# A fused attention and expert kernel whose order is built with other estimates and other weights

## The chip, the cores and the metric

The kernel runs on one core of one Trainium2 chip. The metric is the device time of one execution in microseconds (us). Beside it stands a profile of one execution: what each engine did and when. The engines are PE (matrix multiply; PEld is its loading of weights), DVE (vector), ACT (scalar), POOL (GpSimd) and SP (which issues DMAs here). Each engine takes its instructions in the order in which the program has them; semaphores hold an instruction until what it reads has been written.

## The reference

For 4 batches of 8 heads, 768 positions and 64 channels, attention in which a query sees only keys of the same hash bucket; its output, laid out as 3072 rows of 512, goes through two matrix products with a squared ReLU between them. The core of it:

```python
q_bits = (np.einsum('bhsd,dk->bhsk', q, proj) > 0).astype(np.int64)
k_bits = (np.einsum('bhsd,dk->bhsk', k, proj) > 0).astype(np.int64)
mask = q_bucket[:, :, :, None] == k_bucket[:, :, None, :]
scores = scale * np.matmul(q, k.transpose(0, 1, 3, 2))
scores = np.where(mask, scores, -1000000000.0)
scores = scores - np.max(scores, axis=-1, keepdims=True)
attn = np.exp(scores)
attn = attn / (np.sum(attn, axis=-1, keepdims=True) + 1e-09)
x = np.matmul(attn, v)            # then laid out as (3072, 512)
h = np.maximum(x @ w_in, 0.0)     # (3072, 2048)
out = h * h @ w_out               # (3072, 512)
```

## The kernel before

**The work.** Values that need more than half precision are kept as two f16 parts, a main part and a residual (what is left of the f32 value after the main part); a product is then three matmuls, main by main, main by residual, residual by main. `move` in the code makes a main part, `left` a residual.

*A unit* is 128 queries of one head against its 768 keys. PE writes scores to `pS`; DVE takes the row maximum (`nmx`); ACT takes the exponential with its sum (`e`, `sm`); `rv` is the reciprocal of the sum, one instruction on DVE or POOL and one on DVE; `hl` is the normalised row in two parts, the main one by `move`, the residual by DVE; SP issues a transposing DMA of `hl` into `aT`. Six units (two heads of three) feed one *pair* of attention-value products, `pA` on PE with the values `VV`; its result goes into `xx`, again main part and residual. There are 32 pairs, 192 units.

*An expert stage* takes the four `xx` of 384 rows: for each of 16 blocks of the hidden width 12 matmuls into `pm` (with `win`), a ReLU from `pm` to `g32`, a square in place, the main part of `g` and its residual, and then 9 matmuls into `po` (with `wo`). There are 8 stages. `pm` has one buffer, `g` two. In the first stage the weights `w_in` and `w_out` are still being split into parts, in pieces: `raw` is loaded, `top` and `f` unpack it, `sq` and `pt` find its scale, then come the parts of `win` and `wo`. After the first stage `wo` is scaled in place by `rel`, 16 instructions, before the second stage uses it.

**What sets the order.** The program is not written out in order. Every operation is recorded with the ways in which it can be done (for instance the residual of `g` as a scalar_tensor_tensor on DVE or a tensor_tensor on POOL) and what it depends on. `cost` gives each way a duration in ns, and a planner makes a list schedule of all operations: `forward` starts on each engine what is ready and most urgent, `backward` finds from the schedule how urgent each is, five times over, and the schedule with the shortest planned span is issued. Where an operation has several ways, `forward` compares for each engine when it would be free, plus the operation's cost there times the engine's weight in `PRICE`, plus what is queued ahead; the least wins. DMAs go through one planned queue; a transpose holds SP until the queue is through. DVE and POOL operations that both read the local memory through a shared port are kept apart in the plan (`port`, `held`). In the gaps that the plan leaves on PE before the first expert matmul, `emit` puts filler matmuls (`idle`), one for every 56 ns of 0.6 of the gap. So a number in `cost` or `PRICE` changes which engine does an operation, the order on all engines, and the number of fillers.

Every operation is issued by one line (402; 395 for the fillers, 399 for matmuls recorded as a group), so the profile's rows are told apart by the tiles' names.

Of the kernel before, what the change touches and what calls it, by code (L numbers as in the profile page):

```python
# [13 lines left out]
F32 = mybir.dt.float32  # L14
F32R = mybir.dt.float32r
# [19 lines left out]


BUFS = dict(xx=12, hl=3, raw=2, f=7, e=3, aT=3, g=2, A=2, Q=2, L=2, M=2, RV=2, VV=4)
PRICE = dict(pe=1, dve=3.57, act=0.3, pool=3.06, sp=0.43)
AHEAD, DELAY, LAG = 60, 2500, 1.0

ROUNDS, BEHIND = 4, 40000
# [71 lines left out]
class Program:  # L113
# [59 lines left out]
    @staticmethod  # L173
    def cost(key, name, args, kw):

        size = lambda x: int(np.prod(x.shape[1:]))
        column = {F32: 4 / 2.4, F32R: 0.445}
        if name == "matmuls":

            side = {32: 4, 64: 2}.get(size(args[0][0][1]), 1)  # L180
            t = sum(size(a[2]) * column.get(a[2].dtype, 1 / 2.4) + 7 for a, _ in args) / side
            return t, t
        kinds = [x.rec.kind if isinstance(x, View) else "" for x in args]
        ptr = any(isinstance(x, View) and x.shape[-1] == 1 for x in args[2:3])
        n = max(size(args[0]), size(args[1]) if isinstance(args[1], View) else 0)
        if key == "pe":
            t = max(107, size(args[2]) * column.get(args[2].dtype, 1 / 2.4) + 3)
            return t, t
        if name.startswith("dma"):
            b = int(np.prod(args[0].shape)) * mybir.dt.size(args[0].dtype)  # L190
            inside = name == "dma_start_transpose" or kinds[:2] == ["sb", "sb"]
            busy = 1040 if key == "pool" else (650 if inside else 475) + 50 * (key == "act")
            return busy, b / (175 if name == "dma_start_transpose" else 314)
        if key == "act":
            t = 93 * (isinstance(kw.get("scale"), View) + isinstance(kw.get("bias"), View)) + (51 if "psum" in kinds[:2] else 93) + n / 1.2 + 93 * ("accum_out" in kw)
        elif key == "pool":
            t = 147 + n * (2.1 if args[0].dtype == F32 or args[0].dtype == F32R else 1.88) if name == "tensor_tensor" else 161 + n / 1.2 + 83 * ptr
        else:
            fast = name in ("tensor_copy", "tensor_scalar") and "psum" not in kinds[:2]
            both = len(args) > 3 and isinstance(args[3], View) and args[3].shape[-1] == 1  # L200
            t = 67 + n / (1.92 if fast else 0.96) + 62 * (ptr and (fast or name == "scalar_tensor_tensor")) + 100 * both
        return t, t
# [92 lines left out]
    def forward(self, prio, near):  # L295
# [20 lines left out]
        while True:  # L316
# [25 lines left out]
            if len(o.ways) > 1:  # L342
                for w in o.ways:
                    k2 = w[0].key
                    ahead = sum(ops[j].ways[0][4][0] / len(ops[j].open) for r, j in ready[k2] if ops[j].queue is None and r <= prio[i] + near and j != i)
                    ends[k2] = max(free[k2], t, held if w[5] else 0.0) + w[4][0] * PRICE[k2] + ahead + DELAY * w[1].startswith("dma")
            if any(e < ends[k] and k2 in o.open for k2, e in ends.items()):
# [513 lines left out]
```

## Time and profile before

| | |
|---|---|
| three runs | 923.61, 925.90, 926.62 us, median 925.9 |
| the profiled execution | 925.36 us, of which its span is 923.6 us |
| busy: PE, DVE, ACT, POOL | 885.6, 643.8, 663.6, 54.8 us |
| granted clock of PE, mean | 0.996 |
| first `pm` matmul | starts at 169.50 us |
| last `pA` of the 32 | starts at 822.4 us, last one's matmuls end near 853 |

The span is from the first instruction to the last. A row of groups gives the engine, the operation, what it writes and reads, its shape and count, then after a bar the busy time in us and the mean duration of one in ns, and after a second bar the idle time of that engine just before these instructions, with what ended it. A row of the timeline gives start and duration in us. In the views by stretches each row is one stretch of the span, with its length, then the busy us of PE, PEld, DVE, ACT and POOL, the granted clock, the share of time that DMA packets took, and GB/s. Matmuls are pipelined, and a row's end is modelled; the distance from one start to the next is the better measure of a matmul.

### The profile page before, as it was taken

What the parts mean: (1) busy time and instruction counts of PE and PEld (TensorE: products, weight loads), DVE (VectorE), ACT (ScalarE), POOL (GpSimd) and SP (SyncE); (2) the same over time, 40 slices, a digit from 0 to 9 for tenths busy, and PEclk for the clock granted to TensorE, in tenths of its full rate; (3) what the DMA queues carried; (4) which work ended last, traced back from release to release, by engine and by line L of the source; (5) the groups of instructions that cost most, each with busy time, mean ns of one, the idle gap of its engine ahead of it and who ended that gap; (6) DMA issues with size and microseconds to landing.
All of it is one profiled execution on the core that took longest, in us unless ns stands there. A gap on an engine that the chain in (4) does not pass through costs nothing.

```text
span 923.6 us, 15264 instructions
## 1 busy us (share of the span) xinstructions
PE 885.6 (96%) x5592; PEld 501.3 (54%) x5592; DVE 643.8 (70%) x1206; ACT 663.6 (72%) x1166; POOL 54.8 (6%) x104
## 2 busy tenths in 40 slices
PE   7988988999997999999999999999999999999997
PEld 6555555445554555555555556555555555554553
DVE  5999999988979687889686768797867651211111
ACT  4877987878879677888777768787778673533433
POOL 0111301200103000000000000000000000000000
PEclk9999999999999999999999999999999999999999
DMA  7998999997999797999697959897878640200000
GB/s 236 248 222 210 226 237 213 250 211 193 236 203 242 133 192 148 185 234 244 145 198 159 190 121 198 174 213 154 170 149 177 121 102 10 77 1 0 35 1 35
DMA packets 329323, 149.99 MB, mean 162 GB/s; under 512 B 305568, under 2 KB 305696, under 8 KB 329248
## 3 DMA queue, kind: packets, MB, share of 16 engines
q1 hardware_dynamic: 329248, 149.02, 73.6%
q8 instruction: 44, 0.72, 0.3%
q14 instruction: 31, 0.25, 0.1%
HBM read 43.59 MB, written 6.29 MB: 54 GB/s over the span
## 4 chain that ended last, share of the span: by engine, by line
PE 63%; ACT 5%; DMA 2%; DVE 2%; issue 1%; POOL 0%; SPq 0%; ACTq 0%; DVEq 0%
PE po L402 23%; PE pm L402 21%; PE pS L402 9%; PE pA L399 8%; ACT wo L402 1%; DMA aT<-hl 1%; ACT e L402 1%; PE pd L399 1%; DMA RV<-vp 1%; ACT hl L402 1%; DVE hl L402 1%; ACT g L402 1%; PE pc L402 1%; DVE nmx L402 1%; DMA M<-Q 1%
## 5 line engine op out<-in xcount | busy, mean ns | idle before, releaser
L402 PE MATMUL po<-wo,g 128*128 128x512 f16 x1152 | 332.7, 381 | 2.7 <-ACT wo L402 0.9
L402 PE MATMUL pm<-xx,win 128*128 128x384 f16 x1536 | 322.4, 327 | 1.3 <-DVE g L402 1.0
L402 DVE TENSOR_REDUCE nmx<-pS 128x1 f32<-128x768 f32 x192 | 183.1, 954 | 57.7 <-PE pS L402 56.6
L402 ACT ACTIVATE e<-pS,nmx 128x768 f32<-128x768 f32 x192 | 171.6, 894 | 67.8 <-DVE nmx L402 48.8
L402 DVE SCALAR_TENSOR_TENSOR hl<-e,rv,hl 128x768 f16<-128x768 f32 x192 | 194.1, 1012 | 26.1 <-ACT hl L402 25.5
L402 PEld LDWEIGHTS <-win 128*128 128x128 f16 x1536 | 145.1, 98 | 115.4 <-issue 17.8
L402 ACT ACTIVATE hl<-e,rv 128x768 f16<-128x768 f32 x188 | 173.5, 928 | 25.1 <-ACT e L402 14.0
L402 PEld LDWEIGHTS <-g 128*128 128x128 f16 x1152 | 107.9, 98 | 131.3 <-issue 26.4
L402 DVE SCALAR_TENSOR_TENSOR g<-g,g 128x384 f16<-128x384 f32 x122 | 67.5, 554 | 127.7 <-ACT g L402 127.1
L402 ACT ACTIVATE g<-pm 128x384 f32<-128x384 f32 x125 | 60.7, 486 | 108.3 <-PE pm L402 107.4
L402 ACT ACTIVATE g<-g 128x384 f32<-128x384 f32 (+1 forms) x248 | 128.8, 520 | 10.8 <-PE po L402 5.6
L399 PE MATMUL pA<-aT,VV 128*64 128x384 f16 x1152 | 117.8, 331 | 0.0
L402 PE MATMUL pS<-A,Q 128*128 128x384 f32 x288 | 95.2, 411 | 5.0 <-ACT e L402 4.8
L399 PEld LDWEIGHTS <-VV 128*64 128x64 f16 x1152 | 59.5, 109 | 55.8 <-issue 35.8
L402 PE MATMUL pS<-L,M 128*128 128x384 f32 x288 | 77.8, 350 | 0.2
L402 PEld LDWEIGHTS pS<-A,Q 128*128 128x128 f32 x288 | 49.3, 190 | 29.8 <-ACT e L402 15.9
L402 POOL TENSOR_SCALAR rv<-sm 128x1 f32<-128x1 f32 x74 | 28.8, 389 | 610.6 <-ACT e L402 604.0
L395 PEld LDWEIGHTS <-ones 128*128 128x128 bf16 x756 | 49.9, 103 | 20.1 <-issue 11.8
L395 PE MATMUL idle<-ones 128*128 128x128 bf16 x756 | 54.7, 228 | 2.7 <-DVE ones L402 2.7
L402 PEld LDWEIGHTS pS<-L,M 128*128 128x128 f32 x288 | 51.9, 189 | 3.9 <-issue 2.4
L402 PE MATMUL pS<-Q,M 128*128 128x384 f32 x96 | 37.3, 510 | 9.5 <-ACT e L402 9.1
L402 PE MATMUL pS<-A,L 128*128 128x384 f32 x96 | 36.6, 508 | 5.7 <-ACT e L402 5.4
(92 smaller groups left out, 579.9 us busy)
## 6 DMA issues: line engine op xcount, KB each, us to landing
RV<-vp SPq DMA_DIRECT2D x32, 384.0 KB
R<-kq SPq DMA_DIRECT2D x24, 384.0 KB
raw<-w_in SPq DMA_DIRECT2D x16, 511.8 KB
raw<-w_out SPq DMA_DIRECT2D x16, 511.8 KB
out<-o SPq DMA_DIRECT2D x21, 256.0 KB
Q<-L SPq DMA_DIRECT2D x24, 192.0 KB
Q<-A SPq DMA_DIRECT2D x24, 192.0 KB
L<-M SPq DMA_DIRECT2D x24, 192.0 KB
```

The lines of the kernel that those rows point to most:

```text
L395: issue(q, q.engine.matmul(self.idle[0].real(), self.idle[1].real(), self.idle[1].real(), start=True, stop=True).ins)
L399: ins = q.engine.matmul(*map(real, args), **kw).ins
L402: ins = getattr(q.engine, o.name)(*map(real, o.args), **{k: real(x) for k, x in o.kw.items()}).ins
```

## The change

Four numbers of the planner change: three weights, the bytes per ns of a transposing DMA (175 to 292), and the cost of a POOL operation with one input (161 ns plus 83 for a scale that is a tensor, to 380 ns flat; the part that grows with the size stays).

```diff
-PRICE = dict(pe=1, dve=3.57, act=0.3, pool=3.06, sp=0.43)
+PRICE = dict(pe=1, dve=3, act=1, pool=1.5, sp=0.43)
...
-            return busy, b / (175 if name == "dma_start_transpose" else 314)
+            return busy, b / (292 if name == "dma_start_transpose" else 314)
...
-            t = 147 + n * (2.1 if ... else 1.88) if name == "tensor_tensor" else 161 + n / 1.2 + 83 * ptr
+            t = 147 + n * (2.1 if ... else 1.88) if name == "tensor_tensor" else 380 + n / 1.2
```

What that does to the order is seen on the engines. Three places carry the prediction.

**The end of the first part, on DVE.** Ahead of the sixth `xx` residual, which the first `pm` needs; `top` and `f` unpack weights, `rv` and `hl` are softmax. Before:

```order
L402 SCALAR_TENSOR_TENSOR win<-f,towin,win 128x512 x2
L402 TENSOR_REDUCE nmx<-pS 128x1
L402 SCALAR_TENSOR_TENSOR hl<-e,rv,hl 128x768
L402 SCALAR_TENSOR_TENSOR f<-raw,top_73 128x512
L402 TENSOR_SCALAR top_77<-raw 128x512
L402 RECIPROCAL rv<-rv 128x1
L402 SCALAR_TENSOR_TENSOR xx<-pA,xx 128x384
```

and now:

```order
L402 TENSOR_SCALAR norm<-norm 128x1
L402 SCALAR_TENSOR_TENSOR f<-raw,top_81 128x512
L402 TENSOR_SCALAR norm<-norm 128x1
L402 SCALAR_TENSOR_TENSOR win<-f,towin,win 128x512
L402 TENSOR_SCALAR towo<-norm 128x1
L402 RECIPROCAL rv<-rv 128x1
L402 SCALAR_TENSOR_TENSOR xx<-pA,xx 128x384
```

The `xx` residual was the 304th row of DVE's list (303 instructions and a branch) and is now the 251st; no `top` stands near it, since POOL now has 26 of the 32, where it had 13.

**The scaling of `wo` after the first expert stage.** Before, on ACT, among the exponentials of the next units:

```order
L402 ACTIVATE wo<-wo,rel 128x2x512 x3
L402 ACTIVATE e,sm<-pS,nmx 128x768
...
L402 ACTIVATE wo<-wo,rel 128x2x512
L402 ACTIVATE A<-R,cst 128x768
L402 ACTIVATE hl<-e,rv 128x768
```

and now, on DVE:

```order
L402 TENSOR_SCALAR wo<-wo,rel 128x2x512
L402 RECIPROCAL rv<-rv 128x1
L402 TENSOR_SCALAR wo<-wo,rel 128x2x512 x2
L402 SCALAR_TENSOR_TENSOR hl<-e,rv,hl 128x768
L402 TENSOR_REDUCE nmx<-pS 128x1
```

ACT had 15 of the 16 and DVE one; ACT now has 2, DVE 11 and POOL 3.

**The end of the last stage, on PE.** With the tiles' numbers: the last `pm`, and the `po` matmuls of the last three blocks of the hidden width, each with its own `g`. Before, one `po` of the oldest block and nine of the next stand between the last `pm` and the last block's `g`:

```order
L402 MATMUL pm_10361<-xx_7940,win_726 128x384
...
L402 MATMUL po_9987<-wo_1027,g_10338 128x512
...
L402 MATMUL po_9987<-wo_1027,g_10365 128x512
...
L402 MATMUL po_9987<-wo_1027,g_10386 128x512
```

and now three of the oldest and nine of the next:

```order
L402 MATMUL pm_10143<-xx_7704,win_736 128x384
...
L402 MATMUL po_9767<-wo_1010,g_10122 128x512
L402 LDWEIGHTS g_10122
L402 MATMUL po_9767<-wo_1010,g_10122 128x512
...
L402 MATMUL po_9767<-wo_1010,g_10147 128x512
...
L402 MATMUL po_9767<-wo_1010,g_10168 128x512
```

So PE has two more matmuls to do before it needs the last block's `g`, whose residual is now a tensor_tensor on POOL: 128 of the 128 blocks have it there, where it was 6 (and 122 on DVE).

More of the change, by code (lines that the diff above doesn't have):

```diff
@@ L196, in cost @@
         elif key == "pool":
-            t = 147 + n * (2.1 if args[0].dtype == F32 or args[0].dtype == F32R else 1.88) if name == "tensor_tensor" else 161 + n / 1.2 + 83 * ptr
+            t = 147 + n * (2.1 if args[0].dtype == F32 or args[0].dtype == F32R else 1.88) if name == "tensor_tensor" else 380 + n / 1.2
         else:
```

## The prediction

> **What bounds the kernel now.** I read the page first: busy times, then the two rows that cut the span into 40 slices.
>
> ```profile
> span 923.6 us, 15264 instructions
> PE 885.6 (96%) x5592; PEld 501.3 (54%) x5592; DVE 643.8 (70%) x1206; ACT 663.6 (72%) x1166; POOL 54.8 (6%) x104
> PE   7988988999997999999999999999999999999997
> DVE  5999999988979687889686768797867651211111
> ```
>
> PE looks like the only limit, but its 96% hold two things. The view by stretches, first of all instructions, then of the filler matmuls (tile `idle`) alone, separates them. Columns: length of the stretch, then busy us (and count) of PE, PEld, DVE, ACT, POOL.
>
> ```profile
> 20.00:169.50 149.50, 132.01 (x1084) 82.71 (x1083) 143.20 (x286) 120.54 (x201) 24.64 (x43) 1.00 1.01 229
> 169.50:320.00 150.50, 142.93 (x853) 78.60 (x852) 130.53 (x248) 126.65 (x215) 19.84 (x33) 0.99 0.94 211
> 320.00:900.00 580.00, 577.60 (x3422) 318.29 (x3421) 358.19 (x650) 399.19 (x724) 10.07 (x24) 1.00 0.64 136
> ```
>
> ```profile
> 20.00:169.50 149.50, 42.91 (x631) 1.00 1.01 229
> ```
>
> Up to 169.5 us PE's work is 43 us of filler, and DVE is busy 143.20 of 149.50 us: DVE sets the pace, ACT (120.54) has room. From 320 us on PE is full (577.60 of 580) and DVE has 222 us to spare. Between lies a stretch where both are near full. So the time is (when DVE lets PE get full) plus (what PE still has to do), and an instruction taken from DVE counts only before about 300 us. The timeline shows the hand-over: the sixth `xx` residual on DVE, then the first `pm` matmul on PE.
>
> ```profile
> 168.61 0.53 DVE L402 SCALAR_TENSOR_TENSOR xx<-pA,xx 128x384 f16<-128x384 f32 x1
> 169.06 0.68 DVE L402 SCALAR_TENSOR_TENSOR f<-raw,top 128x512 uint32<-128x512 uint32 x1
> 169.50 1.30 PE L402 MATMUL pm<-xx,win 128*128 128x384 f16 x7
> ```
>
> The rows also show that DVE instructions overlap: 168.61 + 0.53 is 169.14, and the next begins at 169.06. I take 0.05 us off each duration for that.
>
> **The change, part by part.** No arithmetic changes, only who does it and when. The order built from the change has 122 `g` residuals on POOL that were on DVE, 13 more `top` on POOL, 13 more `hl`, 10 of the `wo` scalings moved to DVE, and 216 fewer filler matmuls. The fillers cost nothing themselves: they lie in gaps that DVE makes. The groups' rows price the moves (after the bar: busy us, mean ns):
>
> ```profile
> L402 DVE TENSOR_SCALAR top<-raw 128x512 f16<-128x512 bf16 x19 | 8.8, 463 | 0.4 <-DMA raw<-w_in 0.3
> L402 POOL TENSOR_SCALAR top<-raw 128x512 f16<-128x512 bf16 x13 | 13.4, 1031 | 28.9 <-DMA raw<-w_out 15.3 <-DVE rv L402 6.8 <-DMA raw<-w_in 6.3
> L402 DVE SCALAR_TENSOR_TENSOR g<-g,g 128x384 f16<-128x384 f32 x122 | 67.5, 554 | 127.7 <-ACT g L402 127.1
> L402 POOL TENSOR_TENSOR g<-g,g 128x384 f16<-128x384 f32 x6 | 6.6, 1102 | 10.8 <-ACT g L402 6.0 <-issue 3.7 <-DVE g L402 1.1
> L402 DVE TENSOR_REDUCE rows<-RV 128x12 f32<-128x768 f32 x16 | 15.0, 945 | 6.7 <-ACT RV L402 6.6
> ```
>
> *The first part, DVE's pace.* Up to the sixth `xx` residual DVE's order has 303 instructions before and 250 now. But only the `top` (16 to 5, 11 x 0.463 = 5.1 us) have left the engine; the rest of the 53 (`f`, `win`, `wo` residuals, three units of softmax) is postponed and comes back. So I compare at later points, where the same softmax work is done: at the last `hl` residual that the tenth and the eleventh pair of attention-value products (`pA`) need. At the tenth: 13 `top` fewer (-6.0), 10 `g` residuals fewer (-5.5), `rows` and its like +2.5, small ones +0.3; with 19 overlaps of 0.05 less to take off, -7.8 us. PE's order has by that point 20 more `pm` and 27 more `po` behind it than before, at the steps that these rows show (0.16 and 0.22 us from one start to the next):
>
> ```profile
> 910.05 0.33 PE L402 MATMUL pm<-xx,win 128*128 128x384 f16 x1
> 910.21 0.38 PE L402 MATMUL po<-wo,g 128*128 128x512 f16 x1
> 910.43 0.33 PE L402 MATMUL pm<-xx,win 128*128 128x384 f16 x1
> ```
>
> That is 3.2 + 5.9 = 9.1 us less to do afterwards; together -16.9. At the eleventh: 13 `g` and 13 `top` off, 11 `wo` scalings and 3 `acc` on, -6.2 us; 28 `pm` and 19 `po` ahead, 8.7 us; -14.9. I take the mean, **-15.9**; bounds -20 (nothing is postponed: the 53 instructions' own durations, less the overlaps, sum to 20.4) and -11 (the seventh pair, where the postponed `rows` have come back but few `po` are ahead: -8 and -3).
>
> *The `wo` scalings.* After the first expert stage `wo` is scaled in place, 15 of 16 on ACT:
>
> ```profile
> L402 ACT ACTIVATE wo<-wo,rel 128x1024 f16<-128x1024 f16 x15 | 16.2, 1138 | 0.0
> L402 DVE TENSOR_SCALAR wo<-wo,rel 128x1024 f16<-128x1024 f16 x1 | 0.5, 466 | 0.0
> 260.00:280.00 20.00, 18.34 (x117) 9.85 (x115) 15.29 (x28) 15.77 (x28) 1.63 (x2) 1.00 0.85 193
> 280.00:300.00 20.00, 16.99 (x102) 9.40 (x102) 19.27 (x40) 19.67 (x26) 7.37 (x11) 0.95 1.06 248
> ```
>
> ACT is full there (19.67 of 20) and PE loses 1.66 + 3.01 = 4.7 us, the only real gap after 200 us. Now 11 go to DVE at 0.466, 3 to POOL, 2 stay. I take **-3.5** of the 4.7; bounds 0 and -4.7.
>
> *Port.* 41 wide operations or so come to POOL in the stretch that DVE paces (13 `top`, 14 `g`, the others of `hl`, `A`, `win`, `wo`). When POOL runs, some DVE rows stretch:
>
> ```profile
> 81.50 0.78 POOL L402 TENSOR_SCALAR top<-raw 128x512 f16<-128x512 bf16 x1
> 81.54 1.22 DVE L402 SCALAR_TENSOR_TENSOR wo<-f,towo,wo 128x512 f16<-128x512 f32 x1
> 302.55 1.01 DVE L402 SCALAR_TENSOR_TENSOR hl<-e,rv,hl 128x768 f16<-128x768 f32 x1
> 302.94 1.39 POOL L402 TENSOR_TENSOR g<-g,g 128x384 f16<-128x384 f32 x1 [3.65 <-ACT g L402]
> L402 DVE SCALAR_TENSOR_TENSOR wo<-f,towo,wo 128x512 f16<-128x512 f32 x16 | 12.1, 771 | 0.0
> ```
>
> The `wo` residual that began 0.04 us after POOL took 1.22 instead of 0.77; in the second pair POOL came later and paid itself. I found DVE to be the loser in four of 26 wide POOL operations, some 0.4 us each: 0.065 us an operation, **+2.5** for 41; bounds 0 and +9 (each holds DVE for half its length, half of the time). The Trainium skill's page "SBUF — State Buffer", section "Who interferes with whom", has it as a lock: of GpSimd and a DVE instruction with two SBUF inputs, the one that comes second waits until the other has finished. The rows agree, in both directions.
>
> *`g` residuals, on PE's side.* In the last stages only these stand between `pm` and `po`. The chain after the last matmul of a `pm`:
>
> ```profile
> 907.87 0.49 ACT L402 ACTIVATE g<-pm 128x384 f32<-128x384 f32 x1 [2.29 <-PE pm L402]
> 908.39 1.08 ACT L402 ACTIVATE g<-g 128x384 f32<-128x384 f32 x2
> 909.50 0.56 DVE L402 SCALAR_TENSOR_TENSOR g<-g,g 128x384 f16<-128x384 f32 x1 [3.33 <-ACT g L402]
> 374.65 0.92 POOL L402 TENSOR_TENSOR g<-g,g 128x384 f16<-128x384 f32 x1 [0.22 <-ACT g L402]
> ```
>
> On POOL it takes 0.92 undisturbed, not 0.56, and starts 0.2 later: about 0.55 us late. The order answers with two more `po` matmuls between (front part, last place): 2 x 0.216 = 0.43. Left is 0.1 us for 48 blocks of the last three stages, of which a margin takes most: **+1.5**; bounds 0 and +14 (0.3 each). Behind a late residual PE's whole queue waits. POOL's `rv`, queued behind a `g`, is late by up to 0.92 as well; it is on the path only through the transposes, next.
>
> *Transposes.* Their price falls from 393 KB at 175 bytes/ns (2.25 us) to 292 (1.35 us), so `pA` is put nearer to the unit that feeds it. Three in a row on SP, the `pA` that they feed, and one landing from the chain that ended last:
>
> ```profile
> 408.50 5.21 SPq L402 DMA_TRANSPOSE aT<-hl  x3
> 427.94 0.68 PE L399 MATMUL pA<-aT,VV 128*64 128x384 f16 x6
> 384.29 5.68 DMA aT<-hl
> L399 PE MATMUL pA<-aT,VV 128*64 128x384 f16 x1152 | 117.8, 331 | 0.0
> ```
>
> 5.21/3 = 1.74 us each: the truth lies between the two prices. The last of the three was issued near 412, landed by 418 at the latest, and PE came 10 us later. In the order the PE work between the last score matmul and its `pA` shrinks by up to 9 us for such pairs, so most of that margin goes. I take **+2**; bounds 0 (as before, when `pA` had 0.0 us of idle time ahead of it) and +12 (ten pairs late by 3 x 0.4). The Trainium skill's page "DMA: Bandwidth & Descriptors", section "Latency and other measured facts", gives 261 GB/s for a transpose: 1.51 us as an estimate, also slower than the new price, but by 0.16 instead of 0.39; by it the term would be +1.
>
> Sum: -15.9 - 3.5 + 2.5 + 1.5 + 2 = -13.4. The profiled execution took 925.4 (span 923.6 and 1.8 around it), 0.5 below the median of 925.9: **912 us**.
>
> **Rivals.** *Given back* (921): DVE stays the bound to 320 us, the port takes its +9 and the `wo` scalings load DVE where PE needs it: -11 - 1 + 9 - 1 = -4. For: in 169.5 to 320 DVE is 87% busy, and 11 scalings are added there. Against: DVE loses 0.55 us with every `g`. This is also where the lock rule of the SBUF page would lead if POOL mostly came first.
>
> *Another pace in the head* (924): with DVE lighter, the DMAs hold the units. For: their share is 1.01 in the head. Against: no `pA` waited for one. Then -15.9 falls away, -3.5 + 2 stays.
>
> *Slower* (941): the transposes. PE takes its queue in order; each of the 26 pairs from the sixth on that reaches its `pA` 1.2 us before the tiles land costs 1.2: +31 in place of +2. It decides from 0.6 us a pair on (15.4/26). For: the new price is 0.39 us under the row and three stand in line. Against: margins as that of 10 us.
>
> **How the numbers follow.** Forecast 0.64, its own range 900 to 922 (-25 with the two gains at their ends and no loss; -4 with the losses near theirs); given back 0.14; another pace 0.09; slower 0.13. The range 899 to 926 holds nearly all of the first two and most of the third. What this measurement tells from no change is about 0.3%, 2.8 us. Faster: 0.62 + 0.11 + 0.04 = 0.77; the same 0.08; slower 0.15.
>
> **What would show it.** First `pm` near 150 us (169.5 less the 20 of those 53 instructions), fillers in the proportion of 540 to 756, DVE still above 93% busy until then; `wo` gap in PE under 2 us; DVE `wo`, `win`, `f` residuals with means up by 0.05 to 0.1 us; PE idle before `po` released by POOL `g` under 3 us; `pA` idle time from DMA under 3 us. If `pm` starts near 150 and the span is still over 920, the middle or the transposes took it; if `pm` starts near 165, DVE was not the pace.

## The result, and the profile after

The changed kernel takes **932.8 us** (median of four runs, 932.13 to 933.9); the kernel before takes 925.6 beside it (four runs, 923.61 to 926.62). The ratio is 1.0082 with a 95% interval of 1.0061 to 1.0102: slower by some 7 us, where 13 us faster was forecast. The profiled execution took 933.2 us, of which 931.5 are its span. An execution with a clearly lower granted clock (0.85 or 0.945 where the others have 0.98 to 1.00) is left out of the medians and ratios below.

The head of the page of the changed kernel, its span and the busy times:

```profile
span 931.5 us, 15081 instructions
PE 879.3 (94%) x5375; PEld 487.0 (52%) x5376; DVE 588.2 (63%) x1086; ACT 629.0 (68%) x1117; POOL 211.9 (23%) x273
```

DVE is 56 us lighter and POOL 157 us heavier, as planned. The view by stretches, cut at the first `pm` matmul, which now starts at 153.6 us; then the group of the fillers:

```profile
20.00:153.60 133.60, 118.88 (x851) 69.74 (x850) 121.35 (x227) 106.55 (x180) 34.10 (x58) 0.97 1.09 238
153.60:320.00 166.40, 151.05 (x888) 82.59 (x888) 138.57 (x271) 127.47 (x228) 48.11 (x60) 1.00 0.93 200
320.00:900.00 580.00, 570.53 (x3362) 311.25 (x3361) 318.77 (x571) 374.90 (x679) 123.16 (x144) 1.00 0.64 137
```

```profile
L395 PE MATMUL idle<-ones 128*128 128x128 bf16 x540 | 39.0, 226 | 1.6 <-DVE ones L402 1.6
```

The hand-over comes 16 us earlier. Yet PE stands 15.4 us in the stretch after it (166.40 less 151.05; before 7.6 of 150.50), and 9.5 us from 320 to 900 (before 2.4).

**How far ahead is PE?** Busy time does not answer it, since a matmul that runs alone is booked longer than one in a chain (in the prediction's rows one `pm` alone has 0.33 us, seven in a row 1.30). Counts do. The view by stretches for one tile, from the start to 900 us: first `pm` and `po` before, then the same two after.

```profile
0.00:900.00 900.00, 311.60 (x1488) 1.00 0.76 166
0.00:900.00 900.00, 319.12 (x1104) 1.00 0.76 166
```

```profile
0.00:900.00 900.00, 305.26 (x1464) 0.99 0.76 166
0.00:900.00 900.00, 316.62 (x1086) 0.99 0.76 166
```

At 900 us the change has done 24 `pm` and 18 `po` fewer: 24 x 0.16 + 18 x 0.216 = 7.7 us behind, which is what the spans differ by (7.9). The same count at other times, with 0.30 us for a `pS` matmul and 0.086 for a recorded `pA` (estimates; at 800 and 900 us they play no part, as both kinds are equally far in all rows), gives this table of PE's work ahead of the kernel before (us, each row one profile). The other kernels come below: `half` has lighter transposes, all or some of them, `hl4` a fourth buffer for `hl`, `a` is the change's order and `b` the order before.

| at | 169.5 | 200 | 240 | 280 | 320 | 420 | 600 | 800 | 900 us |
|---|---|---|---|---|---|---|---|---|---|
| the change | 8.3 | 9.4 | 6.0 | 0.7 | 3.4 | -0.8 | -1.3 | -7.2 | -7.7 |
| a_half | 15.5 | 17.3 | 17.6 | 16.4 | 22.6 | 21.4 | 22.5 | 19.5 | 18.0 |
| a_half_first | 17.9 | 19.6 | 20.2 | 18.1 | 24.2 | 19.9 | 17.5 | 12.1 | 11.8 |
| a_half_last | 10.6 | 11.1 | 8.2 | 3.0 | 5.6 | 2.2 | 3.9 | 0.7 | 0.4 |
| a_hl4 | 12.7 | 13.7 | 11.7 | 6.4 | 10.6 | 6.1 | 5.5 | -1.4 | -1.9 |
| b_half | -0.2 | -0.2 | 0.3 | 0.9 | 2.5 | 3.0 | 3.6 | 3.7 | 3.9 |

So the head start of the first row is 8 us and not 16; between 200 and 280 us it goes, and 6 us more go between 600 and 800.

**What stands.** The view of waits (who stood, what it waited for, then total us, times, longest; SPq is SP's queue): before,

```profile
PE pS L402 <- ACT e L402: 19.3, 31, 1.7
ACT hl L402 <- DMA aT<-hl: 1.9, 5, 0.8
SPq L402 <- DMA L<-M: 10.7, 9, 2.1
```

and after:

```profile
PE pS L402 <- ACT e L402: 17.4, 25, 2.8
PE pS L402 <- DMA M<-Q: 7.4, 8, 3.4
PE pA L399 <- DMA aT<-hl: 4.6, 4, 1.7
ACT hl L402 <- DMA aT<-hl: 14.1, 15, 2.6
SPq L402 <- DMA L<-M: 21.0, 15, 4.9
PEld L402 <- POOL g L402: 7.0, 24, 0.6
```

Three waits for a DMA are new or longer. ACT stands before `hl` because the three buffers of `hl` are still being read by transposes; PE stands before the scores because a piece of `M`, which an on-chip send (`M<-Q`) brings on the same SP queue, has not landed; and PE stands before `pA`. All are the queue that carries the transposes. One such place in the timeline, SP and then PE:

```profile
246.60 1.53 SPq L402 DMA_TRANSPOSE aT<-hl  x1
249.17 0.46 SPq L402 DMA_DIRECT2D L<-M  x1
249.72 1.58 SPq L402 DMA_TRANSPOSE aT<-hl  x1
251.36 0.57 SPq L402 DMA_DIRECT2D R<-kq  x1
251.98 0.43 SPq L402 DMA_DIRECT2D RV<-vp  x1
252.51 0.47 SPq L402 DMA_DIRECT2D M<-Q  x1
...
259.29 0.59 PE L402 MATMUL pS<-L,M 128*128 128x384 f32 x2 [3.41 <-DMA M<-Q]
```

`M<-Q` is issued at 252.51 behind a transpose and two loads, and PE's scores that need it start at 259.29, 6.8 us later, after 3.4 us of standing. (The kernel before has one, issued at 245.55 behind a transpose and two loads as well, that landed 5.1 us later.) From 200 to 280 us PE is busy 70.42 us, before 77.06 (first row after, second before):

```profile
200.00:280.00 80.00, 70.42 (x433) 39.31 (x429) 67.99 (x135) 57.61 (x102) 16.94 (x25) 1.00 0.92 188
```

```profile
200.00:280.00 80.00, 77.06 (x466) 43.09 (x464) 69.29 (x132) 66.08 (x116) 6.85 (x14) 1.00 0.94 213
```

The DMA share is no higher (0.92 against 0.94) and fewer bytes move (188 GB/s against 213): there is not more to carry. That it comes at worse moments is what the waits suggest, and not yet shown. None of PE, DVE, ACT and POOL is full: they wait for each other.

### The profile page after: what moved, and what is told of

Same layout as the page of the kernel before. It is cut to its first block, busy times and chain, and to the rows that moved or that the text cites. A ratio compares the mean times of both kernels' runs of the same rounds, so it can differ in the third digit from the quotient of the medians.

```text
span 931.5 us, 15081 instructions
## 1 busy us (share of the span) xinstructions
PE 879.3 (94%) x5375; PEld 487.0 (52%) x5376; DVE 588.2 (63%) x1086; ACT 629.0 (68%) x1117; POOL 211.9 (23%) x273
## 5 line engine op out<-in xcount | busy, mean ns | idle before, releaser
L402 DVE SCALAR_TENSOR_TENSOR hl<-e,rv,hl 128x768 f16<-128x768 f32 x192 | 196.9, 1027 | 33.1 <-ACT hl L402 31.4
L402 POOL TENSOR_TENSOR g<-g,g 128x384 f16<-128x384 f32 x128 | 124.4, 972 | 401.4 <-ACT g L402 249.0
L402 ACT ACTIVATE hl<-e,rv 128x768 f16<-128x768 f32 x176 | 163.0, 930 | 41.1 <-DMA aT<-hl 14.1
L402 ACT ACTIVATE g<-g 128x384 f32<-128x384 f32 (+1 forms) x230 | 119.5, 522 | 11.5 <-PE po L402 3.6
L399 PE MATMUL pA<-aT,VV 128*64 128x384 f16 x1152 | 119.9, 331 | 5.4 <-DMA aT<-hl 4.6
L399 PEld LDWEIGHTS <-VV 128*64 128x64 f16 x1152 | 61.4, 109 | 63.0 <-issue 42.7
L402 DVE SCALAR_TENSOR_TENSOR xx<-pA,xx 128x384 f16<-128x384 f32 x32 | 17.5, 548 | 70.9 <-ACT xx L402 70.7
L402 PE MATMUL pS<-Q,M 128*128 128x384 f32 x96 | 40.0, 539 | 7.9 <-ACT e L402 7.6
L402 DVE TENSOR_SCALAR rv<-sm 128x1 f32<-128x1 f32 x117 | 17.6, 150 | 43.5 <-ACT e L402 40.8
```

Source lines behind the costliest of these rows:

```text
L399: ins = q.engine.matmul(*map(real, args), **kw).ins
L402: ins = getattr(q.engine, o.name)(*map(real, o.args), **{k: real(x) for k, x in o.kw.items()}).ins
```

## The experiments

The theory after this reading: the order's gain is there, and the whole transposes take it back. Rivals: `g` on POOL takes it, or the new numbers simply make a bad order, whatever the transposes do. Each run is compared with runs of the kernel before on the same chip; where two kernels of different rows are compared, it is by their ratios, a hundredth of which is 9.25 us.

### The transposes' price alone

In the change the price goes back to 175, and in the kernel before only the price goes to 292; each builds a new order.

```diff
-            return busy, b / (292 if name == "dma_start_transpose" else 314)
+            return busy, b / (175 if name == "dma_start_transpose" else 314)
```

> The change with the transposes' price put back to 175 bytes per ns; the POOL price and the weights stay as changed, and the g residuals stay on POOL (127 of 128 in this order). Theory A (the cheaper transposes put pA and the sends too close, and the gain of the first part is lost between the sixth and the sixteenth pair): about 915 us, between 908 and 920, PE idle for transposes and sends under 3 us, as before the change. Theory B (POOL: g residuals come late to PE, DVE is locked out): no better than the change, 928 to 936.

> The kernel before with only the transposes' price moved to 292; the g residuals stay on DVE (2 of 128 on POOL). Theory A: slower by 5 to 12 us, 931 to 938, with the waits for transposes that the changed kernel shows (ACT's hl for the transposing DMA 10 us or more, PE's pA 3 us or more). Theory B: the same as before, 923 to 929.

Measured: a_tr175 927.6 us, ratio 1.0037 (1.0022 to 1.0052); b_tr292 943.4, 1.0219 (1.0187 to 1.0250). Waits of b_tr292:

```profile
ACT hl L402 <- DMA aT<-hl: 17.8, 16, 2.2
PE pS L402 <- DMA M<-Q: 5.0, 7, 1.6
```

Alone, the price costs 20 us; in the change it costs 4. Both have the sign that the theory wants, and the same two waits move (with 175 in the change, ACT's falls from 14.1 to 6.1 us and that for `M` from 7.4 to 1.0). But both times lie outside the ranges that the theory gave, a_tr175 outside its rival's too. Even with the price put back nothing of the forecast gain appears, and the two sizes do not agree: what one number costs depends on the others.

### A price between, and the other numbers alone

The change with 226 (so that a transpose costs 1.74 us, what each of three in a row took in the trace of before; the median of all 192 rows on SP is 1.50); the kernel before with only the weights 3, 1 and 1.5; the kernel before with only POOL's 380 ns.

> The change with transposes at 226 bytes per ns, the rate of three in a row in the trace of before (1.74 us each). Theory A: between the change at 292 (933) and at 175 (928), with waits for transposes between theirs. If it is well under both, the right price is the measured one; if it is well over both, the order scatters by more than the price explains.

> The kernel before with only the weights moved to 3, 1, 1.5: all 128 g residuals and all 32 top on POOL, 25 hl too; transposes at 175. Theory A (transposes alone made the change slow, and the POOL moves carry the gain of the first part): 908 to 920. Theory C (moving so much to POOL costs by itself, because what comes back from it is late or DVE is locked out, about as much as it saves): 922 to 932, with PE's matmuls waiting for POOL's g for 7 us or more in all.

> The kernel before with only the price of one-input POOL operations moved to 380 ns: 2 top and 9 g on POOL, 43 rv there instead of 74. Both theories: little moves, 920 to 930; theory A has it a little slower than before, since DVE gets 11 top back in the part that it paces (about +4), theory C the same or faster.

Measured: a_tr226 953.4, 1.0314 (1.0281 to 1.0346), slower than with either neighbour; b_price 933.6, 1.0104 (1.0061 to 1.0147); b_pool380 925.2, 1.0009 (0.9993 to 1.0024). Waits of a_tr226:

```profile
ACT hl L402 <- DMA aT<-hl: 31.8, 28, 3.6
PE pS L402 <- DMA M<-Q: 11.6, 10, 2.4
```

With that the simple form of the theory, a price below the measured one costs and the measured one mends it, has fallen. A price of 175, 226 and 292 gives 927.6, 953.4 and 932.8: every new number makes another order, and these scatter by more than the effect looked for. Nor do the parts add up: POOL's price alone does nothing, the weights alone cost 9.6 us and the transposes' price 20, all of them together 7.6. What the weights alone cost is not explained here: b_price has the transposes at 175, and its waits for them are smaller (ACT's `hl` 5.3 us, PE's scores for `M` 3.7). From here on the order is held fixed.

### The order held fixed, the transposes made light

The change's order and the order before, unchanged on every engine; each transpose moves only the main half of the row (192 KB instead of 384), so the residual of the softmax rows is left out of the products, whose count stays.

```diff
+            if o.name == "dma_start_transpose":
+                args = [args[0][:, 0:KC], args[1][:, 0:S]]
...
-aTs[h][:, c]
+aTs[h][:, c % KC]
```

> The changed kernel with its planned order untouched, but each transposing DMA moves only the main part of hl, half of the bytes; the products that should read the residual's half read the main part's again, so the residual of the softmax is left out. Theory A: the order's own gain shows once the transposes are cheap in fact: 905 to 915, at least 15 us under the change. Theory B: 925 to 932, since POOL and PE do the same work in the same order.

> The kernel before, its order untouched, with the same half transposes (the residual of the softmax is left out). Both theories: its order left enough room for the transposes, so little is gained: 918 to 925. If it gains as much as the changed kernel does, transposes are a load on both and not what tells them apart.

Measured: a_half **906.1 us, 0.9806** (0.9783 to 0.9830); b_half 920.4, 0.9955 (0.9940 to 0.9970). Lines of a_half: the first stretch up to its first `pm`, the stretch in which the head start was lost, and what is left of ACT's wait.

```profile
20.00:144.40 124.40, 114.31 (x851) 67.39 (x849) 121.04 (x224) 105.30 (x179) 35.36 (x58) 1.00 0.90 199
200.00:280.00 80.00, 75.94 (x468) 42.92 (x463) 72.61 (x140) 66.06 (x118) 21.58 (x29) 1.00 0.66 149
```

```profile
ACT hl L405 <- DMA aT<-hl: 1.2, 3, 0.6
```

This is the experiment that settles most. Between the two light kernels the change's order is 1.5% better, 13.8 us: the gain exists. Whole transposes instead of halved ones cost the change 1.0082 - 0.9806, that is 25.5 us (26.7 by the medians), and the order before 4.2. DVE is busy 97% of the time in the light head (121.04 of 124.40), 91% in the change's own (121.35 of 133.60): there DVE does not set the pace any more, it waits.

### Where in the run

The change's order; transposes light in the first 16 pairs only, or in the last 16 only (the residual is left out in those).

```diff
+light = lambda n: n < 16        # the other: n >= 16
...
+            if o.name == "dma_start_transpose" and light(turn.index(i) // 6):
+                args = [args[0][:, 0:KC], args[1][:, 0:S]]
```

> The change's order, unchanged on every engine; the transposes of the first 16 of the 32 pairs move only the main half of the row (the residual of the softmax rows is left out of those products), those of the last 16 are whole. All halved it took 906.1, none 932.8. If the transposes cost their 26.7 us while the head, the middle and the weights' loads share the queue with them (the head start of 16 us was gone by the 17th pair), this takes 909 to 914, and the last pairs alone 926 to 930. If they cost evenly by pair, 919 here. If it is the tail, where PE is full and has nothing else to do, 926 or more.

> The counterpart: the change's order, transposes of the first 16 pairs whole, of the last 16 only the main half (that residual is left out). First half to blame: 926 to 930. Evenly: 919. Tail: 912 or less. If the two runs' gains add up to much less than 26.7 us, the last pairs make good what the first lost only when they are light too.

Measured: a_half_first 913.6, 0.9876 (0.9856 to 0.9896), 19.1 us under the change; a_half_last 924.9, 0.9997 (0.9976 to 1.0018), 7.9 under it, a little more than expected. The two add up to 27 of the 25.5, so the parts are nearly independent, and the first, up to about 400 us, carries seven tenths. In the table above a_half_first loses 12 of its 24 us from 320 us on (its transposes become whole before 420); a_half loses 5 there.

### `g` on POOL

The change's order, with each residual of `g` issued to DVE in its place; whole transposes, then light ones (residual of the softmax left out). The edit, shortened:

```diff
+            if q is self.pool and o.name == "tensor_tensor" and o.args[3] is ALU.subtract:
+                q = self.dve    # scalar_tensor_tensor(x0, x1, 1.0, x2, mult, subtract)
```

> The changed kernel with its planned order untouched, but every g residual that stands on POOL is issued on DVE, at the same place of the order. Theory A: POOL's latency is not what makes the change slow, so 928 to 936. Theory C: PE's waits for POOL's g (7.0 us) go, and with them up to 7 us: 924 to 928; DVE gets 68 us of work back, most of it after 300 us where it has room.

> The changed kernel's order with half transposes (the residual of the softmax left out, as in the run of that kind before) and every g residual issued on DVE at its place. If the move of the g residuals to POOL carries part of the gain once transposes are out of the way, this is slower than the 906 of the half transposes alone: by 6 to 12 us where the first part's sum is right (13 g in the stretch that DVE paces, and DVE in their way in all stages up to 320 us). If the rest of the order carries it: 903 to 909.

Measured: a_gdve 934.1, 1.0104 (1.0076 to 1.0132); a_half_gdve 911.0, 0.9851 (0.9836 to 0.9867), against 0.9806 with `g` on POOL. Waits of a_gdve:

```profile
ACT hl L408 <- DMA aT<-hl: 13.7, 15, 2.7
PE pS L408 <- DMA M<-Q: 6.2, 7, 2.0
PEld L408 <- DVE g L405: 2.1, 2, 1.7
```

The 7.0 us that PE's weight loads stood for POOL's `g` are gone (2.1 us for DVE's `g` in their place), and the time is not better; the DMA waits are as they were. With light transposes `g` on POOL is worth 4 us, between the two ranges expected. For the `g` residuals that rival falls; the other operations moved to POOL were not moved back with the order fixed.

### A fourth buffer for the normalised row

The order fixed, `hl` gets a fourth buffer (two constants share one with `acc` to make room); then the same with the fourth buffer in the plan too, so that the order is built anew.

```diff
-tag=tag or name, bufs=bufs)
+tag={"o": "acc"}.get(tag, tag or name), bufs=bufs + (name == "hl"))
```

> The changed kernel with its planned order untouched on every engine, but with four hl buffers in memory where the plan knows three (the room comes from two constants that share a buffer with acc). ACT's hl then no longer waits for the transpose that reads the buffer's last content. Theory A1 (late transposes do their harm through that ring: ACT stands, then the exponentials, then PE's scores): ACT's 14.1 us of waits go below 3 and the time falls by 8 to 18 us, to 915 to 925. Theory A2 (they do it at pA and at the sends queued behind them on SP, the ring is beside the point): 928 to 933.

> The kernel before, its order untouched, with the same fourth hl buffer. Both theories: ACT waited 1.9 us for transposes in it, so 920 to 926.

> The change with four hl buffers in the plan and in memory, so the order is made anew. Theory A1: 905 to 920, under both kernels, with ACT's waits for transposes under 5 us. Theory A2: 925 to 935.

Measured: a_hl4 928.8, 1.0053 (1.0035 to 1.0070); b_hl4 923.8, 0.9997 (0.9980 to 1.0014); a_plan4 951.2, 1.0291 (1.0235 to 1.0347). Waits of a_hl4:

```profile
ACT hl L402 <- DMA aT<-hl: 2.8, 2, 1.5
PE pS L402 <- DMA M<-Q: 10.0, 9, 3.3
PE pA L399 <- DMA aT<-hl: 6.8, 4, 2.6
```

ACT's 14.1 us of standing become 2.8, and 2.7 us of them come out at the end by the ratios (4.0 by the medians; the ten runs of a_hl4 scatter from 925.6 to 933.8). PE stands longer for `M` and `pA` instead (16.8 us for 12.0). The ring of buffers is one of the places, not the cause. In the table above the profiled run of a_hl4 (928.0) is 4 to 7 us ahead of the change all along, and still loses much as the change does: 7 us between 200 and 280, 7 between 600 and 800. The newly planned order with the same room is 22 us slower than the fixed one, another case of that scatter.

### The sends' place on SP's queue

The change's order with only the on-chip sends moved: ahead of up to two transposes where what they read is already issued (a_sends), or, where no transpose stands between a send and an earlier send that it waits for, behind the next one (a_apart1); each also with the fourth buffer. The first edit, shortened:

```diff
+            if o.name == "dma_start" and (both tiles are on the chip):
+                passed = (transposes between its last dependency and itself)[-2:]
+                if passed:
+                    out.remove(i)
+                    out.insert(passed[0], i)
```

> The change's order, with one thing moved: each on-chip send (the pieces of Q, A, L and M) goes ahead of up to two transposes on SP's queue, as far as what it reads is already issued; some 33 sends move, most by one transpose. In the change's profile PE stood 7.4 us for M that such sends brought. If the sends' place behind the transposes is what costs, those 7.4 us go and with them 5 to 8 us of the time: 925 to 928. If the sends are late because the DMA engines are busy, or because M itself comes late, nothing: 931 to 935; and if the transposes that are passed are as urgent, slower, up to 938.

> The same sends moved, and a fourth buffer for the normalised row, which alone gave 928.8. If the two losses are separate, 921 to 924, at or under the kernel before. If the time that one gives is taken by the other wait (with the fourth buffer PE's standing for M grew from 7.4 to 10.0 us), 927 to 930.

> The opposite of the run that moved the sends ahead (970.5; SP stood 82 us before sends that wait for an earlier send to land, after 35 in the change and 17 in the kernel before): the change's order, where each on-chip send that reads or overwrites what an earlier send moves goes behind the next transpose if no transpose stands between the two, as far as what reads it allows; some ten of 48 move. If SP's standing with transposes queued behind it is what costs, that standing falls by 8 to 15 us, ACT's and PE's standing for aT with it, and the time is 925 to 930. If the later sends are paid by PE, which waits for M (7.4 us in the change), 931 to 938. If only the pace of DMA counts, 932 to 934.

> The same sends behind the next transpose, with a fourth buffer for the normalised row, which alone gave 928.8 with 10.0 us of PE's standing for M and 35 us of SP's for earlier sends. If SP's standing costs, 920 to 925, at or under the kernel before; if PE pays for the later M, 929 to 935.

Measured: a_sends 970.5, 1.0486 (1.0449 to 1.0522); a_sends_hl4 955.2, 1.0329 (1.0308 to 1.0351); a_apart1 948.5, 1.0255 (1.0230 to 1.0280); a_apart1_hl4 942.8, 1.0187 (1.0134 to 1.0241). All four are outside what was expected, the first two by far; of the last two the rival had the sign and the payer, PE, and too small a price. Waits of a_sends:

```profile
SPq L412 <- DMA L<-M: 55.1, 23, 3.8
ACT hl L412 <- DMA aT<-hl: 56.1, 31, 5.2
PE pA L409 <- DMA aT<-hl: 14.2, 5, 4.3
PE pS L412 <- DMA M<-Q: 3.2, 4, 1.3
```

and of a_apart1:

```profile
SPq L416 <- DMA L<-M: 17.4, 11, 3.8
PE pS L416 <- DMA M<-Q: 14.2, 9, 3.7
PE pS L416 <- DMA A<-A: 4.2, 2, 2.5
ACT hl L416 <- DMA aT<-hl: 11.0, 12, 2.2
```

Ahead, PE gets its `M` sooner (3.2 us of standing for 7.4), but a send that waits for the landing of an earlier one (`M<-Q` for `L<-M`) holds SP, and with it every transpose behind: 55 us, and ACT stands 56. Behind, SP stands less (17.4 for 21.0), the transposes are sooner, and PE pays for `M` (14.2 and 4.2). Moving some thirty sends forward by a place or so costs 37 us, moving about ten back costs 16. So the queue is on the critical path with both its kinds of passenger. It does not show that SP's standing is what the change lost: taking some of it away did not help, since the send that is late then is as urgent, and a_half, 25 us faster, still has SP standing 17.9 us for `L<-M`.

No kernel with whole transposes beats the kernel before by more than the measurement tells; b_hl4 and b_pool380 equal it.

## Why the prediction was wrong, step by step

**The step that failed is the term "Transposes", "I take +2; bounds 0 and +12".** With the order fixed, whole transposes instead of halved ones cost the change 25.5 us and the kernel before 4.2: the term is **+21**, outside its bounds. With it in place of +2 the forecast's sum becomes +6; 7 was measured. Without the term the sum was -15.4, and the light kernels show -13.8. That these two agree is in part luck: by the table a_half is 20.1 us ahead of b_half at 320 us, where -15.9, -3.5 and +2.5 make 16.9, and then loses 6.0 of them by 900 us, where the forecast had +1.5.

The working went wrong in two ways. It looked at one reader of a transpose, `pA`, and at the margin of one pair (10 us in the quoted rows). In the change PE's standing before `pA` is 4.6 us: at that place the forecast was nearly right, and "under 3 us" missed by little. It left out who else waits for the queue. Transposes give back the `hl` buffers that ACT needs (14.1 us of standing, some 3 of them at the end), and the sends that carry `Q`, `A`, `L` and `M` stand in the same line, ahead of PE's scores (7.4 us). The other way was to price a pair's lateness at `pA` alone and sum over pairs; what was lost is the pace of the units.

**DVE's pace, -15.9.** Right as a statement on the order, wrong as one on the kernel. With light transposes PE is 15.5 us ahead at 169.5 us; in the change 8.3. The expected sign "DVE above 93% busy until then" would have shown it: 97% in the light kernel, 91% in the change, where the DMA share in that stretch is 1.09 (light 0.90, before 1.01). The first `pm` near 150 us (153.6) and the fillers (540) came out as said, and prove little: the sixth `xx` needs few units, and the units were the ones that were late.

**The `wo` scalings, -3.5.** This term was too large. The 16 scalings run at another time in each kernel; from the first one's start to the end of the last, before, in the change and in a_half:

```profile
275.90:297.80 21.90, 17.26 (x110) 9.97 (x109) 21.38 (x39) 21.80 (x28) 8.81 (x12) 1.00 1.05 240
257.30:284.80 27.50, 21.25 (x129) 11.72 (x130) 21.24 (x36) 17.69 (x32) 6.70 (x11) 1.00 1.01 207
246.50:269.10 22.60, 19.73 (x123) 10.88 (x124) 19.71 (x36) 17.53 (x32) 7.75 (x11) 1.00 0.75 160
```

ACT is no longer full there, but PE loses 6.3 us in the change, before 4.6; 3.4 of the 6.3 are the wait for `M` shown above. With light transposes PE loses 2.9. So the term is -1.7 when the queue is out of the way, and nothing is gained in the change; "under 2 us" is not reached in either.

**Port, +2.5.** The right size. The groups of DVE after:

```profile
L402 DVE SCALAR_TENSOR_TENSOR wo<-f,towo,wo 128x512 f16<-128x512 f32 x16 | 13.0, 826 | 1.2 <-ACT wo L402 1.2
L402 DVE SCALAR_TENSOR_TENSOR win<-f,towin,win 128x512 f16<-128x512 f32 x16 | 13.0, 812 | 0.0
L402 DVE SCALAR_TENSOR_TENSOR hl<-e,rv,hl 128x768 f16<-128x768 f32 x192 | 196.9, 1027 | 33.1 <-ACT hl L402 31.4 <-POOL hl L402 1.4
```

`wo` went from 771 to 826 ns, `win` from 770 to 812, `hl` from 1012 to 1027: 0.9 + 0.7 + 2.8 us over the whole run (the term was for the part that DVE paces), and `f`, expected to lengthen too, did not (687 ns after, 694 before). Single instructions double on either side:

```profile
L402 DVE SCALAR_TENSOR_TENSOR wo<-f,towo,wo x16: 733/744/1351, 80.8 to 209.6; 128x512 f16<-128x512 f32 x16
L402 POOL TENSOR_SCALAR top<-raw x26: 761/772/1612, 38.0 to 195.6; 128x512 f16<-128x512 bf16 x26
```

By shortest, median and longest, a `wo` on DVE pays up to 0.6 us and a `top` on POOL up to 0.8. That the one that comes second pays is what the prediction's two pairs of rows show, but not by all that is left of the first: DVE's `wo` lost 0.45 us there where POOL's `top` had 0.74 to go. When both start within 0.05 us it can be the first: a DVE `hl` at 199.51 us took 1.77, with a `g` on POOL from 199.56. The Trainium skill's page "SBUF — State Buffer", section "Who interferes with whom", has it that the order of issue decides who is blocked; pairs that start further apart agree (a DVE `hl` 0.23 us behind a `top` at 63.71 took 1.29).

**`g` residuals, +1.5.** PE's weight loads stood 7.0 us for them, more than the "under 3 us" said, but that is not on the path: a_gdve takes it away and gains nothing, and in the light kernels, where they stand 8.3 us, `g` on POOL gains 4 us.

**The rivals.** "Slower" named the transposes as its culprit and the price of 292 as its reason, and its sign came true; its mechanism, 26 pairs each 1.2 us late at `pA`, did not. "Another pace in the head" had half the truth: with DVE lighter the DMAs hold the units, which takes 7 of the 16 us (15.5 less 8.3 at 169.5 us); what spoke against it, "no `pA` waited for one", again counted one reader only. It was given 0.09 and "Slower" 0.13, as if they were two causes; halving the transposes removes both.

**What stays open.** How the 21 us divide between ACT's `hl`, the sends and `pA`: some 3 are shown for the buffers; taking away any single wait moved the standing to another. Halving a transpose both frees SP's queue sooner and takes bytes off the DMA engines (their share from 200 to 280 us falls from 0.92 to 0.66); no run tells the two apart, though moving sends without a byte more shows that the order on the queue alone can cost more than the term. That the price of 292 is to blame is shown for the kernel before alone (20 us); within the change it is 4 us, and the rest comes with the order that all four numbers make together. From 600 to 800 us the change loses 6 us and a_half 3, which b_half does not; halving the transposes does not remove those 3, and their cause is open.

## What to carry to other kernels

When one engine is made lighter, list everything that waits for the next resource, not only the consumer that comes to mind: here one DMA queue served ACT's buffers, the operands of PE's scores and those of `pA`, and in the kernel before, where DVE set the pace, halving its transposes was worth only 4 us. A planner's number changes the whole order, so test its parts with the order held fixed and one resource made light; new orders scattered by 25 us here, more than the effect. A margin read in the trace of before belongs to the pace of before.

## What was not expected of the hardware

SP's queue is so tight that the place of single sends decides: 37 us slower by moving some thirty of them ahead of a transpose, without a byte more to carry. A send on the chip of 192 KB that stands behind a transpose and two loads took 6.8 us from its issue to the first matmul that uses it, and 5.1 us from issue to landing in the kernel before.

PE's clock dips in the head of the change. Two neighbouring stretches of 10 us; the granted clock is the third number from the right:

```profile
50.00:60.00 10.00, 6.86 (x46) 4.14 (x43) 7.95 (x17) 7.53 (x15) 3.00 (x6) 0.99 1.21 205
60.00:70.00 10.00, 9.68 (x63) 5.77 (x65) 8.62 (x16) 7.96 (x14) 1.77 (x5) 0.84 1.11 252
```

After a slice with PE busy for 6.86 of 10 us the next has a clock of 0.84; the slice from 80 us has 0.83, after one with 8.04 (the kernel before had 1.00 in every such slice from 20 to 170 us). The Trainium skill's page "TensorE: Matmul & The Clock Gate", in its part on the clock gate, has a gate that passes half the pulses for a window of 3.4 us after an idle one; as an estimate from that page a slice of 10 us with one such window has a mean of 0.83. The trace agrees with the size of the dip. It does not show an idle window of that length: PE's longest gap there is 2.76 us, before 60.06. The number of fillers does not explain the dips: a_half issues the same fillers in the same places of the order and has one slice below 1.00 after 20 us (0.94). What these dips cost is not known: PE was not the pace there.
